# A new head for a fused attention and expert kernel: another order of loads, gates, decays and scores, fillers spread among them, and scores' operands loaded in two parts

## The chip, the core and the metric

The kernel runs on one core of a Trainium2 chip. The core has a matrix engine (TensorE, PE in the profile), three engines for elementwise work (VectorE or DVE, ScalarE or ACT, GpSimd or POOL), a queue that issues transfers (SyncE or SP) and 16 DMA engines. Each engine works through its own list of instructions in order and waits on semaphores for the others. The metric is the time of one execution on the device in microseconds; less is better.

## What is computed

A recurrent attention with gates (2 batches, 8 heads, 768 steps, head size 40) feeds two expert layers in a row, all in float32:

```python
for t in range(S):
    m_new = np.maximum(f_gate[:, :, t] + m, i_gate[:, :, t])
    f_stab = np.exp(f_gate[:, :, t] + m - m_new)
    i_stab = np.exp(i_gate[:, :, t] - m_new)
    m = m_new
    C = f_stab * C + i_stab * einsum('bhd,bhe->bhde', vt, kt)
    n = f_stab * n + i_stab * kt
    y[:, :, t] = sigmoid(o_gate) * (C q_t) / max(|n q_t|, 1)
x = y as 1536 rows of 320
x = ((x @ w_a) * (x @ w_b)) @ w_out      # inner width 1536
out = leaky_relu(x @ w_in) @ w_out2      # inner width 2048
```

The expert weights arrive as float64 and are turned into float32 pieces on the chip.

## The kernel before

The steps of attention are cut into 6 chunks of 128 for each of the 2 batches; a chunk is written `p:b`. Within a chunk the recurrence becomes matrix products: scores (k times q, `score_mm`, step `smm`), a matrix of decays (`decay_scan`, step `dsc`), their product (`score_at`, `sat`), outputs (`out`), and the state carried on (`state_mm`, `stm`). The decays of chunk 0 come from the gates: two scans (`gate_scan`), sums and differences (`gate_fa`, `gate_fb`, `gate_i`), exponentials (`gate_exp`), a split of the result in two parts (`gate_first`), and products that spread a row over all partitions (`decay_mm`, `dmm`). `gate_cums` (`gcum`) makes running products for the later chunks; `store_decays` and `store_cums` write them to memory, from where the later chunks read them.

The outputs are divided by a denominator (`outputs_norm`, three small DVE instructions, step `onm`), multiplied by the output gate (`gate_norm` on POOL, step `og`; `norm` on DVE, step `nrm`), transposed on PE (`x_mm`, step `xmm`) and split into a high part (`x_hi` on ACT, `xh`) and a rest (`x_lo` on DVE, `xl`).

A weight is loaded (`load_raw`, `lw`), decoded from float64 by two ACT instructions (`dh`, `dl`) and a merge on DVE (`dm`), rounded on ACT (`dr`), and its rest taken on POOL (`ds`). The first expert layer then runs in 12 slices: the two up products (`up`, line 559), their product split in two parts (`e1`, `em`, `eh`, `el`), and the down product (`dn`, lines 617 to 619). The second layer does the same with `um`, `v1`, `vh`, `vl` and `dd` (lines 586 and 617 to 619).

Nothing is scheduled by the compiler. The string `ORDER` lists 1116 steps, and each engine's instructions stand in the order in which these steps issue them. `spin` is a step without a result: one product of zeros, 128x512 in bfloat16, which only keeps PE running. Before, 16 of them stand at the start. Each tile pool in the PSUM memory has a few buffers, and a step that needs a buffer waits until its last reader is done: `ps_att` chooses among three pools, `pa` (2 buffers), `mm` (2) and `dn` (4).

Of the kernel before, what the change touches and what calls it, by code (L numbers as in the profile page):

```python
# [7 lines left out]
F32 = mybir.dt.float32  # L8
# [10 lines left out]
B, H, S, D = 2, 8, 768, 40  # L19
# [5 lines left out]
T = 128  # L25
# [12 lines left out]
    dm:2 onm:0:1 dm:4 out:0:0 lc:1 lf:1:0 lw:3 scum dr:4 og:0:1 smm:1:0 dsc:1:0:1 onm:0:0 dh:3 dr:2 dsc:1:0:0
    og:0:0 lw:6 lk:1:0 lq:1:0 ld:1:0 stm:0:0 stm:0:1 ds:4 sat:1:0:0 nrm:0:1 nrm:0:0 lf:1:1 sat:1:0:1 dl:3
    ste:0:1 nd:0:0 ds:2 val:1:0 ste:0:0 nd:0:1 vo:1:0 xmm:0:0 xmm:0:1 xh:0:0 lk:1:1 lw:5 ls:1:1 lw:7 lq:1:1  # L40
    ld:1:1 xh:0:1 xl:0:0 xl:0:1 up:0:1 up:0:0 dm:3 dl:6 dh:6 qry:1:0 dr:3 e1:0:1 e1:0:0 dm:6 em:0:1 em:0:0
    sig:1:0 eh:0:0 eh:0:1 out:1:0 ds:3 el:0:1 onm:1:0 el:0:0 dsc:1:1:1 up:0:3 dr:6 dh:5 sig:1:1 dl:5 val:1:1
    og:1:0 ds:6 vo:1:1 qry:1:1 dm:5 up:0:2 lw:8 e1:0:3 nrm:1:0 em:0:3 dsc:1:1:0 e1:0:2 dn:0:0 smm:1:1 dh:7 dl:7
    dr:5 nd:1:0 sat:1:1:0 sat:1:1:1 em:0:2 dm:7 lk:2:0 lq:2:0 lw:9 eh:0:2 up:0:4 lf:2:0 dl:8 dr:7 eh:0:3 out:1:1
    xmm:1:0 dh:8 key:1:0 ds:5 onm:1:1 dn:0:1 el:0:2 el:0:3 dn:0:2 og:1:1 xh:1:0 e1:0:4 nrm:1:1 xl:1:0 em:0:4
    dm:8 ds:7 dn:0:3 nd:1:1 stm:1:0 xmm:1:1 eh:0:4 dl:9 xh:1:1 up:0:5 dr:8 xl:1:1 ste:1:0 ds:8 e1:0:5 up:1:0
    em:0:5 el:0:4 lw:10 ls:2:0 lk:2:1 vo:2:1 val:2:0 key:1:1 up:1:1 smm:2:0 dh:9 eh:0:5 e1:1:0 dsc:2:0:0 dm:9
# [5 lines left out]
    out:2:0 eh:1:5 dh:13 dr:11 eh:0:6 dr:12 sig:2:0 el:1:5 dsc:3:0:1 e1:0:7 up:1:6 onm:2:0 em:0:7 key:2:1
    ste:2:0 el:0:6 e1:1:6 eh:0:7 dl:13 ds:12 ds:11 val:2:1 og:2:0 up:1:7 dn:0:6 dn:1:5 el:0:7 em:1:6 nrm:2:0
    dm:13 smm:2:1 qry:2:1 stk:1:1 lw:14 lw:16 lf:3:1 up:0:8 dl:15 e1:1:7 eh:1:6 dr:13 sat:2:1:0 dl:14 dh:14
    el:1:6 stk:2:0 ds:13 dl:16 nd:2:0 em:1:7 sat:2:1:1 eh:1:7 dh:15 e1:0:8 dsc:3:1:0 dn:1:6 out:2:1 dn:0:7
    up:0:9 em:0:8 el:1:7 dm:14 dn:1:7 dm:15 stm:2:1 onm:2:1 dsc:3:1:1 dr:14 up:1:8 e1:0:9 eh:0:8 dr:15 og:2:1
# [66 lines left out]
def attention_experts_kernel(ctx: ExitStack, tc: tile.TileContext, gates, consts, stk, kvo, q3, w1, wd1, w2, wd2, out):  # L124
# [35 lines left out]
    idr = c_p.tile([128, 4, 128], F32, name="idr")  # L160
# [173 lines left out]
    def decay_mm(b, hh):  # L334
        p = 0
# [467 lines left out]
```

## Time and profile before

| | |
|---|---|
| median of 3 runs | 456.62 us (456.11 to 456.94) |
| the profiled execution | 455.65 us, of which the span of the engines' work is 453.9 us |
| PE busy, share of the span | 98% |
| DVE, ACT, POOL busy | 46%, 46%, 28% |
| transfers | 47.79 MB, mean 105 GB/s |

A row of the timeline gives the start and the length in microseconds, the engine, the line of the kernel, the operation, the tile written and the tiles read, the shapes and the count; brackets hold the idle time before it and what ended that. A matrix product in float32 may appear as two records (16 of line 372 are 8 products). PE's granted clock is given as a share of its full speed: 1.00 is 2.4 GHz, 0.50 is 1.2 GHz. Before the first change of the clock the table shows 1.00 for want of a record.

### The profile page before, as it was taken

To read this page: it belongs to the slowest core of one execution; us is meant where nothing else is said; L and a number is where in the kernel's file an instruction comes from. 1 tells how busy PE (TensorE), PEld (TensorE's weight loads), DVE (VectorE), ACT (ScalarE), POOL (GpSimd) and SP (SyncE) were. 2 spreads that over 40 slices of the span, in tenths; PEclk is the share of its full clock that TensorE was granted. 3 is DMA by queue.
4 is the path that set the end of the run, shared out by engine and by line. 5 is a ranking of instruction groups with operands and counts; after the bars stand their busy time and mean duration, and the time that the engine had idled before them with its cause. 6 is when DMAs were issued, how large, how long until landed. Compare 5 with 4: busy or idle time off the path is not lost.

```text
span 453.9 us, 7049 instructions
## 1 busy us (share of the span) xinstructions
PE 446.4 (98%) x2774; PEld 404.5 (89%) x2774; DVE 209.3 (46%) x352; ACT 208.2 (46%) x381; POOL 125.5 (28%) x135
## 2 busy tenths in 40 slices
PE   7999999999999999999999999999999999999997
PEld 3989999999988898898888888989899999999896
DVE  5997978677565453343156431342422131131112
ACT  4776756645142223125676655843533343333222
POOL 2678582964412611010314241030300000000000
PEclk9569999999999999999999999999999999999999
DMA  7999997862460410015412534010010000010001
GB/s 245 308 356 289 279 269 219 279 182 57 136 188 27 135 32 2 0 39 241 139 59 63 181 89 155 1 58 1 0 59 0 2 0 1 1 59 0 1 0 59
DMA packets 25998, 47.79 MB, mean 105 GB/s; under 512 B 1801, under 2 KB 18765, under 8 KB 25965
## 3 DMA queue, kind: packets, MB, share of 16 engines
q1 hardware_dynamic: 25965, 47.34, 33.7%
q8 instruction: 22, 0.36, 0.3%
q14 instruction: 11, 0.09, 0.1%
HBM read 45.28 MB, written 2.05 MB: 104 GB/s over the span
## 4 chain that ended last, share of the span: by engine, by line
PE 96%; DMA 1%; DVE 1%; ACT 1%; SPq 0%; issue 0%; POOL 0%; ACTq 0%
PE mm L559 30%; PE mm L586 20%; PE dn L617 11%; PE dn L619 11%; PE dn L618 11%; PE pa L419 4%; PE pa L372 3%; PE pa L414 2%; PE dn L419 2%; PE pa L445 1%; DMA ident_all<-consts 1%; PE pa L490 1%; PE pa L649 1%; PE mm L445 1%; PE dn L372 0%; PE pa L340 0%
## 5 line engine op out<-in xcount | busy, mean ns | idle before, releaser
L559 PE MATMUL mm<-xh,wa 128*128 128x256 f32 (+1 forms) x480 | 114.8, 340 | 0.6 <-ACT xh L504 0.6
L559 PEld LDWEIGHTS mm<-xh,wa 128*128 128x128 f32 x480 | 79.8, 189 | 9.6 <-ACT xh L504 0.8
L602 DVE TENSOR_TENSOR gl<-gg,gh 128x512 fp32r<-128x512 f32 x48 | 34.2, 730 | 99.4 <-ACT gh L597 95.3
L559 PE MATMUL mm<-xl,wa 128*128 128x256 f32 (+1 forms) x288 | 79.3, 337 | 0.0
L592 ACT ACTIVATE gg<-mm 128x512 f32<-128x512 f32 x48 | 28.1, 594 | 72.3 <-PE mm L586 70.9
L617 PE MATMUL dn<-wa,gh 128*128 128x320 f32 x192 | 59.5, 310 | 0.0
L619 PE MATMUL dn<-wa,gl 128*128 128x320 f32 x192 | 59.3, 309 | 0.0
L618 PE MATMUL dn<-wa,gh 128*128 128x320 f32 x192 | 59.2, 309 | 0.0
L559 PEld LDWEIGHTS mm<-xl,wa 128*128 128x128 f32 x288 | 51.1, 189 | 6.0
L564 ACT ACTIVATE gg<-mm 128x256 f32<-128x256 f32 (+1 forms) x48 | 23.4, 487 | 67.0 <-PE mm L559 51.1
L569 DVE TENSOR_TENSOR gg<-gg,mm 128x256 f32<-128x256 f32 (+1 forms) x48 | 26.2, 546 | 59.4 <-PE mm L559 35.3
L617 PE MATMUL dn<-wd,gh 128*128 128x320 f32 x144 | 45.9, 319 | 0.0
L619 PE MATMUL dn<-wd,gl 128*128 128x320 f32 x144 | 44.5, 309 | 0.0
L618 PE MATMUL dn<-wd,gh 128*128 128x320 f32 x144 | 44.4, 309 | 0.0
L578 DVE TENSOR_TENSOR gl<-gg,gh 128x256 fp32r<-128x256 f32 (+1 forms) x48 | 36.0, 753 | 11.7 <-ACT gh L573 11.6
L573 ACT ACTIVATE gh<-gg 128x256 fp32r<-128x256 f32 (+1 forms) x48 | 25.0, 522 | 32.4 <-DVE gg L569 25.4
L597 ACT ACTIVATE gh<-gg 128x512 fp32r<-128x512 f32 x48 | 29.8, 630 | 21.7 <-PE dn L618 21.3
L618 PEld LDWEIGHTS dn<-wa,gh 128*128 128x128 f32 x192 | 36.1, 188 | 1.3
L617 PEld LDWEIGHTS dn<-wa,gh 128*128 128x128 f32 x192 | 36.0, 188 | 1.2
L619 PEld LDWEIGHTS dn<-wa,gl 128*128 128x128 f32 x192 | 36.0, 188 | 0.0
L586 PE MATMUL mm<-yh,wa 128*128 128x512 f32 x120 | 35.8, 395 | 0.0
L586 PE MATMUL mm<-yh,w 128*128 128x512 f32 x120 | 35.6, 394 | 0.0
(110 smaller groups left out, 739.2 us busy)
## 6 DMA issues: line engine op xcount, KB each, us to landing
y<-w SPq DMA_DIRECT2D x12, 768.0 KB
raw<-w SPq DMA_DIRECT2D x8, 768.0 KB
kvo<-kvo SPq DMA_DIRECT2D x12, 484.0 KB
pp<-fdr SPq DMA_DIRECT2D x10, 512.0 KB
raw<-wd SPq DMA_DIRECT2D x8, 640.0 KB
stk<-stk SPq DMA_DIRECT2D x12, 416.0 KB
y<-wd SPq DMA_DIRECT2D x6, 640.0 KB
out<-y SPq DMA_DIRECT2D x12, 160.0 KB
```

The lines of the kernel that those rows point to most:

```text
L419: pe.matmul(ps[:, h * E1:(h + 1) * E1], at_t[p, b, h // 4][:, h % 4, :], v[:, h, :], start=p == 0, stop=p == 0 or h == h0 + nh - 1,)
L559: pe.matmul(halves_[ab], w[:, slot, ab, :], xs[lo][:, kt, cs], start=i == 0, stop=i == 7)
L569: dve.tensor_tensor(out=g, in0=g, in1=up_t.pop((blk, f))[1], op=ALU.mult)
L573: act.activation(out=gh, in_=g_t[blk, f], func=AF.Copy)
L578: dve.tensor_tensor(out=gl, in0=g_t.pop((blk, f)), in1=raw_view(gh_t[1, blk, f]), op=ALU.subtract)
L586: pe.matmul(ps, w[:, slot, f % 2, :], xs[lo][:, kt, :], start=i == 0, stop=i == 7)
L592: act.activation(out=g, in_=ps, func=AF.Prelu, alpha=0.01)
L597: act.activation(out=gh, in_=g_t[2, blk, f], func=AF.Copy)
L602: dve.tensor_tensor(out=gl, in0=g_t.pop((2, blk, f)), in1=raw_view(gh_t[2, blk, f]), op=ALU.subtract)
L617: pe.matmul(ps, gh[:, cs], w[:, 0, :], start=f == 0, stop=False)
L618: pe.matmul(ps, gh[:, cs], w[:, 1, :], start=False, stop=False)
L619: pe.matmul(ps, gl[:, cs], w[:, 0, :], start=False, stop=f == last)
```

## The change

The step table is replaced by one of 1151 steps. The 16 `spin` steps at the start become 51, of which 15 stand before the first transpose and the rest among the products of the head. Gates and decays of chunk 0 now stand ahead of the weights' merges, batch 0 ahead of batch 1; `gcum` stands behind the first two products of scores and decays. The tile of a chunk's scores operands holds two groups of 40 partitions, at 0 and at 64. It was one transfer of 104 partitions, the 24 between them filled with zeros by the host's layout; it becomes two transfers of 40. The steps `gate_ist`, `decay_mm` and `state_mm` take their PSUM buffers from other pools, and so does the fillers' target. The order of all later steps differs too.

```diff
-    lg:0 init spin spin spin spin spin spin spin spin spin spin spin spin spin spin spin spin lg:1 lw:1 lc:0
-    ls:0:1 gs:0 lw:0 lk:0:1 ls:0:0 lw:2 gfa:0 gs:1 gfa:1 sel gfb:0 gfb:1 gi:0 smm:0:1 gi:1 dh:1 idr gef:1 gef:0
+    lg:0 lg:1 lw:0 init gs:0 gfa:0 gfb:0 gi:0 gei:0 gef:0 lc:0 gfr gs:1 gi:1 spin dh:0 gfa:1 dl:0 idr sel spin
+    spin spin spin spin spin spin spin spin spin spin spin spin spin gist:0 ls:0:0 lk:0:1 spin spin dmm:0:0 spin
...
     def load_stk(p, b):
         t = a_p.tile([128, 2, 4, T], F32, tag="stk", name="stk", bufs=3)
-        sp.dma_start(out=t[0:64 + D], in_=stk[b, p])
+        for u in range(2):
+            sp.dma_start(out=t[64 * u:64 * u + D], in_=stk[b, p, u])
         stk_t[p, b] = t
...
     def gate_ist(cc, n):
-        ps = ps_att("mm")
+        ps = ps_att()
...
     def decay_mm(b, hh):
-            src = ps_att("mm" if b and hh else None)
+            src = ps_att()
...
     def state_mm(p, b):
-        ps = ps_att(None if p else "mm")
+        ps = ps_att(None if p else "dn")
...
-    wps = ps_dn.tile([128, 512], F32, tag="dn", name="dn")
+    wps = ps_mm.tile([128, 512], F32, tag="mm", name="mm")
...
-    stk = np.zeros((B, NC, 64 + D, 2, 4, T), np.float32)
-    for u in range(2):
-        stk[:, :, 64 * u:64 * u + D] = qk[:, :, u].transpose(1, 3, 5, 0, 2, 4)
+    stk = qk.transpose(1, 4, 2, 6, 0, 3, 5)
```

Lines of the changed kernel are higher by 1 to 3 (372 becomes 375, 559 becomes 562).

DVE, from the second gate scan on, before: the selector (line 691), the gates' differences (284, 288), the running products (308), the copy of the input gates (323), a weight's merge (231), then scans of the decays (350) and products with the scores (377).

```order
L691 TENSOR_TENSOR sel<-ident_all 64x16
L284 TENSOR_TENSOR wd<-wd 64x128
L284 TENSOR_TENSOR wd<-wd 16x640
L288 TENSOR_TENSOR wd<-wd 16x128
L288 TENSOR_TENSOR wd<-wd 16x640
L308 SCALAR_TENSOR_TENSOR wd<-wd,zero 16x128 x5
L323 COPY istn<-mm 128x16
L231 SCALAR_TENSOR_TENSOR y<-y 128x768
L350 SCALAR_TENSOR_TENSOR pp<-pa,idr 128x512
```

The same place in the changed kernel:

```order
L694 TENSOR_TENSOR sel<-ident_all 64x16
L326 COPY istn<-pa 128x16
L234 SCALAR_TENSOR_TENSOR y<-y 128x768
L287 TENSOR_TENSOR wd<-wd 16x640
L353 SCALAR_TENSOR_TENSOR pp<-pa,idr 128x512 x2
L380 TENSOR_TENSOR at<-dn,pp 128x512 x2
L311 SCALAR_TENSOR_TENSOR wd<-wd,zero 16x128 x5
L353 SCALAR_TENSOR_TENSOR pp<-pa,idr 128x512
```

Of the gates' differences only the long one of the decays is still behind the selector, the merge stands ahead of it, and the five running products stand behind two scans and two products.

PE from the last fillers to the first up product, before: scores (372), input gates (322), decays (340), outputs (419), states (445), transposes (490).

```order
L372 MATMUL dn<-stk 128x128 x8
L322 MATMUL mm<-ident_all,wd 128x16
L340 MATMUL mm<-fr,sel 128x128 x4
L340 MATMUL pa<-fr,sel 128x128 x12
L322 MATMUL mm<-ident_all,wd 128x16 x5
L372 MATMUL dn<-stk 128x128 x8
L419 MATMUL dn<-kvo,at 128x41 x16
L372 MATMUL pa<-stk 128x128 x8
L445 MATMUL mm<-kvo 120x123 x2
...
L490 MATMUL pa<-ident_all,ya 128x128 x6
L559 MATMUL mm<-xh,wa 128x256 x4
```

PE in the changed kernel, from the last transposes of the head on; a pair with `gg` is one filler:

```order
L493 MATMUL pa<-ident_all,ya 128x128 x3
L448 MATMUL dn<-kvo 120x123 x2
L448 MATMUL dn<-kvo 80x82
L331 LDWEIGHTS gg
L331 MATMUL mm<-gg 128x512
L562 MATMUL mm<-xh,wa 128x256 x4
...
L331 LDWEIGHTS gg
L331 MATMUL mm<-gg 128x512
L375 MATMUL pa<-stk 128x128 x8
```

The scores of chunk 1:0 (the third row of 372, now 375) have moved from ahead of the states to behind the first up product, and a filler stands on either side of that product.

DVE at the outputs of chunk 1:1 in the changed kernel, where PE goes from the last output products (422) straight to a down product (620 to 622) that reads this `gl`:

```order
L433 TENSOR_SCALAR den<-pa 128x8
L434 TENSOR_TENSOR den<-den,pa 128x8
L435 RECIPROCAL rec<-den 128x8
L581 TENSOR_TENSOR gl<-gg,gh 128x256
L481 TENSOR_TENSOR ya<-pa,kvo 128x320
```

And PE there, in the changed kernel and then before:

```order
L422 MATMUL pa<-kvo,at 128x41 x2
L620 MATMUL dn<-wd,gh 128x320
L621 MATMUL dn<-wd,gh 128x320
L622 MATMUL dn<-wd,gl 128x320
```

```order
L419 MATMUL pa<-kvo,at 128x41 x2
L490 MATMUL pa<-ident_all,ya 128x128 x3
L617 MATMUL dn<-wd,gh 128x320
L618 MATMUL dn<-wd,gh 128x320
L619 MATMUL dn<-wd,gl 128x320
```

Before, the down products right behind the outputs are those of slice 1 (`dn:0:1`), and those of slice 2 follow; now slice 1 stands earlier, and slice 2 (`dn:0:2`) comes straight behind the outputs.

## Rows read from the trace of the kernel before

**Rows 1.** The page: busy us, share of the span and instructions of each engine.

```profile
PE 446.4 (98%) x2774; PEld 404.5 (89%) x2774; DVE 209.3 (46%) x352; ACT 208.2 (46%) x381; POOL 125.5 (28%) x135
```

**Rows 2.** Windows: length, each engine's busy us, granted clock, DMA share, GB/s.

```profile
9.88:30.36 20.48, 19.83 (x112) 18.57 (x110) 18.81 (x33) 14.49 (x22) 12.99 (x18) 0.50 1.02 331
30.36:100.00 69.64, 69.04 (x580) 67.78 (x580) 54.26 (x97) 44.70 (x85) 49.20 (x48) 1.00 0.87 257
```

**Rows 3.** Windows: the stretch between the fillers and the first scores.

```profile
7.30:9.17 1.87, 0.00 (x0) 0.00 (x1) 1.82 (x5) 1.83 (x4) 0.11 (x1) 1.00 0.98 283
```

**Rows 4.** Timeline of PE, from the first filler to the first up product.

```profile
1.00 6.28 PE L328 MATMUL dn<-gg 128*128 128x512 bf16 x16 [1.00 <-DVE wd L688]
...
9.17 1.53 PE L372 MATMUL dn<-stk 40*128 40x128 f32 x16 [1.90 <-DMA stk<-stk]
...
11.16 1.11 PE L340 MATMUL mm<-fr,sel 64*128 64x128 f32 x4 [0.19 <-POOL fr L296]
...
18.12 7.05 PE L419 MATMUL dn<-kvo,at 128*128 128x41 f32 x32
25.10 2.08 PE L372 MATMUL pa<-stk 40*128 40x128 f32 x16
27.11 2.60 PE L445 MATMUL mm<-kvo 128*120 128x123 f32 x12
...
31.32 0.74 PE L559 MATMUL mm<-xh,wa 128*128 128x256 f32 x4 [0.60 <-ACT xh L504]
```

**Rows 5.** Timeline of DVE in the head.

```profile
7.35 0.17 DVE L691 TENSOR_TENSOR sel<-ident_all 64x16 fp32r<-64x16 f32 x1 [1.55 <-DMA ident_all<-consts]
7.45 1.01 DVE L284 TENSOR_TENSOR wd<-wd 64x128 f32<-64x128 f32 x2
...
9.32 1.91 DVE L308 TENSOR_TENSOR_SCAN wd<-wd,zero 16x128 f32<-16x128 f32 x5
...
11.22 0.94 DVE L231 SCALAR_TENSOR_TENSOR y<-y 128x768 int32<-128x768 int32 x1
13.16 1.22 DVE L350 TENSOR_TENSOR_SCAN pp<-pa,idr 128x512 f32<-128x512 f32 x1 [1.00 <-PE pa L340]
...
20.71 0.69 DVE L377 TENSOR_TENSOR at<-dn,pp 128x512 f32<-128x512 f32 x1
```

**Rows 6.** Timeline of ACT in the head.

```profile
7.03 0.90 ACT L223 ACTIVATE y<-y 128x768 f32<-128x768 f32 x1 [5.00 <-DMA y<-w]
7.83 0.61 ACT L696 ACTIVATE idr<-ident_all 128x512 f32<-128x512 f32 x1
...
12.19 0.89 ACT L240 ACTIVATE wa<-y 128x768 fp32r<-128x768 f32 x1 [0.18 <-DVE y L231]
...
22.65 0.83 ACT L401 ACTIVATE kvo<-kvo 128x320 f32<-128x320 f32 x2
...
30.39 0.87 ACT L504 ACTIVATE xh<-pa 128x384 fp32r<-128x384 f32 x2 [1.16 <-PE pa L490]
```

**Rows 7.** Timeline of POOL: the output gates of chunks 0:1 and 0:0.

```profile
23.27 1.27 POOL L437 TENSOR_TENSOR kvo<-kvo,rec 128x320 f32<-128x320 f32 x1 [1.33 <-DVE rec L432]
26.26 1.46 POOL L437 TENSOR_TENSOR kvo<-kvo,rec 128x320 f32<-128x320 f32 x1 [1.72 <-DMA ddr<-wd]
```

**Rows 8.** Timeline of PE at the full clock: scores of chunk 1:1, last outputs of 1:1.

```profile
42.72 1.16 PE L372 MATMUL pa<-stk 40*128 40x128 f32 x16
...
47.79 0.57 PE L419 MATMUL pa<-kvo,at 128*128 128x41 f32 x4
```

**Rows 9.** Timeline of DVE around those outputs.

```profile
45.72 2.38 DVE L231 SCALAR_TENSOR_TENSOR y<-y 128x768 int32<-128x768 int32 x1
48.40 0.17 DVE L430 TENSOR_SCALAR den<-pa 128x8 f32<-128x8 f32 x1 [0.30 <-PE pa L419]
...
48.92 1.24 DVE L578 TENSOR_TENSOR gl<-gg,gh 128x256 fp32r<-128x256 f32 x2
50.08 0.48 DVE L478 TENSOR_TENSOR ya<-pa,kvo 128x320 f32<-128x320 f32 x1
```

More of the change, by code (lines that the diff above doesn't have):

```diff
@@ L38 @@
[L38 to L47, printed above, removed]
@@ L53 @@
[L53 to L57, printed above, removed]
@@ new lines @@
+    out:0:1 key:0:1 val:1:0 og:0:0 vo:1:0 onm:0:1 dr:1 dh:4 dl:4 dr:2 spin spin spin spin stm:0:1 spin og:0:1
+    spin lw:3 scum spin nrm:0:0 lf:1:0 lq:1:0 lc:1 ld:1:0 ls:1:0 nrm:0:1 dm:4 nd:0:1 dl:3 nd:0:0 ds:1 xmm:0:0
+    spin xmm:0:1 stm:0:0 spin dr:4 dsc:1:0:0 sig:1:0 xh:0:0 xh:0:1 dh:3 xl:0:0 xl:0:1 ste:0:0 dm:3 up:0:0 spin
+    dr:3 e1:0:0 lw:6 ds:2 lf:1:1 smm:1:0 dsc:1:0:1 sat:1:0:0 em:0:0 sat:1:0:1 qry:1:0 ds:4 up:0:1 dh:6 dl:6
+    eh:0:0 e1:0:1 out:1:0 ds:3 dsc:1:1:0 dsc:1:1:1 lk:1:1 lw:5 onm:1:0 em:0:1 dm:6 dl:5 og:1:0 vo:1:1 val:1:1
@@ new lines @@
+    sig:1:1 el:0:0 dr:6 eh:0:1 up:0:3 lq:1:1 ls:1:1 ds:6 nrm:1:0 up:0:2 dn:0:0 smm:1:1 e1:0:3 nd:1:0 el:0:1
+    key:1:0 em:0:3 lw:7 ld:1:1 sat:1:1:0 ste:0:1 e1:0:2 eh:0:3 dl:7 dh:5 dh:7 dn:0:1 xmm:1:0 up:0:4 el:0:3
+    em:0:2 sat:1:1:1 dm:5 dm:7 dr:5 eh:0:2 xh:1:0 dr:7 e1:0:4 qry:1:1 out:1:1 ds:5 xl:1:0 onm:1:1 el:0:2 og:1:1
+    lw:8 nrm:1:1 ds:7 dn:0:2 nd:1:1 dh:8 dl:8 dn:0:3 stm:1:0 xmm:1:1 up:0:5 ste:1:0 em:0:4 dm:8 xh:1:1 eh:0:4
+    dr:8 lw:9 ls:2:0 lf:2:0 lk:2:0 lw:10 xl:1:1 e1:0:5 up:1:0 el:0:4 em:0:5 stk:1:0 ds:8 key:1:1 up:1:1 dl:9
@@ new lines @@
+    nd:2:0 dh:16 e1:0:9 dr:15 stm:2:1 out:2:1 em:0:9 el:0:8 onm:2:1 ste:2:1 eh:0:9 dl:16 ds:14 og:2:1 up:1:8
+    dn:0:8 xmm:2:0 up:1:9 xh:2:0 dsc:3:0:0 nrm:2:1 el:0:9 nd:2:1 e1:1:8 xmm:2:1 dn:1:7 ds:15 em:1:8 xl:2:0
+    up:0:10 lk:3:1 lq:3:0 ld:3:1 qry:3:0 lf:4:0 lq:3:1 dn:0:9 dh:17 eh:1:8 e1:1:9 xh:2:1 el:1:8 em:1:9 ls:3:1
+    lk:4:0 dm:17 xl:2:1 dm:16 eh:1:9 e1:0:10 em:0:10 dr:16 smm:3:0 up:1:10 el:1:9 sat:3:0:1 sat:3:0:0 eh:0:10
+    dr:17 e1:1:10 dn:1:8 stk:2:0 ds:16 key:3:0 vo:4:0 vo:3:1 out:3:0 up:1:11 sig:3:1 em:1:10 ls:4:0 dsc:3:1:0
@@ new lines @@
+    el:0:10 onm:3:0 og:3:0 eh:1:10 e1:1:11 nrm:3:0 smm:3:1 dn:1:9 up:0:11 dsc:3:1:1 em:1:11 sat:3:1:0 el:1:10
+    sat:3:1:1 stm:3:0 stk:2:1 val:3:1 qry:3:1 dsc:4:0:0 ste:3:0 key:3:1 ds:17 e1:0:11 out:3:1 eh:1:11 nd:3:0
+    onm:3:1 og:3:1 nrm:3:1 ls:5:1 lk:4:1 lq:4:0 dn:1:10 ld:4:0 xmm:3:0 dn:0:10 xh:3:0 nd:3:1 el:1:11 em:0:11
+    xl:3:0 xmm:3:1 eh:0:11 xh:3:1 xl:3:1 dn:1:11 stm:3:1 dsc:4:0:1 ste:3:1 up:2:0 lq:4:1 lk:5:0 ls:4:1 lf:4:1
+    e1:2:0 el:0:11 em:2:0 dn:0:11 smm:4:0 stk:3:0 val:4:0 val:5:0 qry:4:0 key:4:0 up:2:1 eh:2:0 ye:0 sig:4:0
@@ new lines @@
+    ye:1 e1:2:1 sat:4:0:0 el:2:0 sat:4:0:1 em:2:1 stm:4:0 out:4:0 up:2:2 dn:2:0 e1:2:2 eh:2:1 el:2:1 dsc:4:1:1
+    ste:4:0 onm:4:0 em:2:2 lq:5:0 lf:5:0 up:2:3 dn:2:1 vo:4:1 og:4:0 stk:3:1 stk:4:0 e1:2:3 eh:2:2 nrm:4:0
+    em:2:3 dsc:4:1:0 el:2:2 up:2:4 dn:2:2 smm:4:1 ls:5:0 ld:4:1 lk:5:1 ld:5:0 lf:5:1 val:4:1 key:4:1 vo:5:1
+    qry:4:1 eh:2:3 sig:4:1 e1:2:4 sat:4:1:1 em:2:4 el:2:3 sat:4:1:0 eh:2:4 nd:4:0 up:2:5 xmm:4:0 xh:4:0 e1:2:5
+    em:2:5 out:4:1 el:2:4 dsc:5:0:0 onm:4:1 up:2:6 dn:2:3 og:4:1 vo:5:0 e1:2:6 eh:2:5 xl:4:0 em:2:6 el:2:5
@@ L108 @@
+    dd:2:14:3 dd:2:15:3
 """
```

107 lines of the change are left out of this document (49 added, 58 removed).

## The prediction, made before the changed kernel had run

> **What bounds the kernel now.** I read the page first: PE is busy 98% of the span and no other engine is above 46% [rows 1]. So the time is PE's list of work, its clock, and the few places where PE waits. The windows come next. From 9.88 to 30.36 us PE is busy 19.83 of 20.48 us, yet at a granted clock of 0.50, the level of 1.2 GHz; from 30.36 to 100 it is busy 69.04 of 69.64 us at 1.00 [rows 2]. Ahead of that PE stood idle from 7.30 to 9.17, for 1.87 us, and the clock fell at 9.88 [rows 3]. The timeline of PE shows what this slow head holds: 16 fillers to 7.28, then a wait of 1.90 us for the first scores' operands, decays, scores, outputs for 7.05 us from 18.12, scores of chunk 1:0 for 2.08, states for 2.60, and the first up product at 31.32, behind a last wait of 0.60 for `xh` [rows 4]. Behind that product PE hardly waits. The kernel is therefore a head of 31.32 us and a body of full PE at the full clock, and whatever moves the first up product moves the end by as much, unless the body gains or loses something of its own.
>
> What holds the head? DVE's timeline: the first scan of decays (line 350) starts at 13.16, after a wait of 1.00 for PE's decay products, and the last product of scores and decays (377) ends at 20.71 + 0.69 = 21.40 [rows 5]. From there to 31.32 PE works off outputs, scores, states and transposes at half clock.
>
> **The change: the chain up to the first scan.** Ahead of everything ACT waits 5.00 us for the first weight, which lands at 7.03 [rows 6]. The change has the gates and one weight of the same size ahead there still, so I leave 7.03 for `lw:0`, the weight whose merge now stands ahead of the first scan on DVE. Two decoding instructions of at most 0.90 each on ACT [rows 6] overlap by some 0.10, so they end near 8.7; the copy `idr`, 0.61, ends at 9.3 and is hidden behind the merge, 0.94 on DVE [rows 5], which ends near 9.6. Then comes the long gate difference: the pair on line 284 takes 1.01 [rows 5], of which I give 0.8 to the one of 640 columns (all 1.01 is the upper bound). First scan: 10.4 in place of 13.16.
>
> **Up to the last product of the head.** From 13.16 to 21.40, 8.24 us, DVE does four scans of 1.22, four products of 0.69, a merge and a small copy, close together [rows 5]. The changed list holds the same between its first scan and its last product, and in addition the five running products, 1.91 us [rows 5], which stood ahead before. 10.4 + 8.24 + 1.91 = 20.5, against 21.40: only 0.9 us of the 2.8 is left at this point. PE must keep up: at the full clock I halve what it does in rows 4 (a filler, 6.28 / 16 = 0.39 at the start, becomes 0.2 as an estimate; the scores at full clock have a row, 1.16 [rows 8], where one chunk took 2.08 [rows 4]). Scores of two chunks, decays, outputs of 3.5 and the fillers between then fit beside DVE's list, and the wait of a decay product for a PSUM buffer still held by a scan is inside DVE's time.
>
> **From there to the first up product.** Now PE's work is behind other engines. A denominator takes 0.52 on DVE, from 48.40 to 48.92 [rows 9]; the list has two of them around a merge of 0.9, to 22.4. The output products in between are four, about 0.8 at most before the second denominator, beside the merge. POOL multiplies the output gates in 1.27 and 1.46 [rows 7]; I take 1.2 behind the second denominator, since nothing but small steps stands ahead of it on POOL: 23.6. The normalizing product on DVE, 0.48 [rows 9]: 24.0. Then ACT's list is what ends last: a merge of 0.94 on DVE must go ahead, 24.9; a rounding of 0.89 on ACT, 25.8; one sigmoid, 0.83 / 2 = 0.42, 26.2; two `xh`, 0.87 together, 27.1 [rows 5, 6, 9]. With a little for semaphores the first up product starts at 27.2, where it was 31.32: **-4.1**. States, transposes and fillers of PE lie beside this chain.
>
> **Given back.** The scores of chunk 1:0 have left the head and stand behind the first up product, at the full clock: 1.16 [rows 8], **+1.1**. The fillers on either side of that product: one on the path, **+0.2**. The first up product's `xl` part waits for `x_lo`, which follows `x_hi`: **+0.2**. Further on, at the outputs of chunk 1:1, PE goes straight from the outputs to a down product that reads a `gl`. On DVE that `gl` stands behind the denominators of the same outputs, so PE must wait for the end of its own outputs, then 0.52 of denominators and one `gl`, 1.24 / 2 = 0.62 [rows 9], and two semaphores; the two products of `gh` ahead of it cover some 0.3. Before, transposes and an earlier slice filled this place. Behind the waiting product stand the rest of slice 2 and the states: **+1.0**. Sum: -4.1 + 1.1 + 0.2 + 0.2 + 1.0 = **-1.6**.
>
> **The load in two parts.** Twelve loads of operands, 4 KB for each partition, carry 320 KB each in place of 416, so DMA moves 12 x 96 KB = 1.15 MB less of 47.79. In the head, where DMA's share is 1.02 at 331 GB/s [rows 2], 96 KB is 0.3 us, some 0.4 with the second load of the head, at most. The other bound is nothing: in the stretch in which such a load was moving, DMA's share was 0.98 but the rate 283 GB/s [rows 3], so such a load doesn't fill the engines it is spread over. I take nothing, since the first scores' place in the new chain is behind `dm:0` and the decays, which don't wait for this load. The Trainium skill, "DMA: Bandwidth & Descriptors", in its section on why a DMA increments its semaphore by 16, says that a transfer is spread over the largest number up to 16 that divides its partitions, on the lowest-numbered engines: 104 partitions would use 13 engines with 8 rows each, 40 use 10, and both parts the same ten, again 8 rows each. By this the two parts land no sooner and the sum stays -1.6; by bytes it is -2.0. The lower rate of that stretch agrees with it as far as it goes.
>
> The order of all later steps differs too. PE's instructions there are the same ones, and 98% busy leaves them little to win; I put nothing, and up to 3 us of loss as a rival.
>
> **The rivals.** (A) The sum: -1.6. On the profiled execution, 455.65, that is 454.05, a span of 452.3; the median shown is 0.97 above the profiled time, so the median is **455.0**. Its own range, with the bounds of loads and differences and the wait at slice 2 between 0 and 2: 454.0 to 455.8.
>
> (B) The clock falls in the thin stretch from the last outputs to the first up product, where PE has fillers, states and transposes in place of solid work. For it: it fell after 1.87 us of idling [rows 3]. Against: the fillers break the idle time up. If it stays at half until about 30.4 as before [rows 2], the up products from 27.2 on run at half for 3.2 us and lose 1.6: 456.6, no change.
>
> (C) The other side. The clock falls before the scores, as it did, and PE's longer list, now with fillers, binds. After 9.88 it holds some 34 fillers at 0.39, 13.3 us, and the products of the old head, 19.83 [rows 2] plus 0.7 of scores ahead of it less 2.08 for chunk 1:0, 18.4: 32 us in all at half. At half to 30.36, 20.5 of these are done; the rest takes 6 at the full clock: first up at 36.4 in place of 31.32, with the 2.5 given back behind it about +7, 463. It decides from about 3 us of half clock on at a place where PE binds. Against it: the first decay products need only the gates, not the scores' operands for which PE waited 1.90 [rows 4], and fillers stand in that gap.
>
> (D) The body loses more. Merges on DVE beside other work take 2.38 [rows 9] where the first took 0.94 [rows 5]; weights loaded later (the second is now issued behind four other loads) come later through decode, merge and rounding, and each up product that waits costs its wait. One to 3 us: 457 to 458.
>
> (E) It goes better: no wait at slice 2, as DVE is far ahead there (-2.6), or POOL's product is off the path as well (-3.4): 453.2 to 454.0.
>
> **How the numbers follow.** A 0.46, B 0.20, C 0.10, D 0.14, E 0.10. What can be told from no change here is about 0.2%, 0.9 us. The range leaves out C and little of D: 453.2 to 458.0. Faster by over 0.2% (below 455.7): nearly all of A and E, 0.52. Within it: B, the lower end of D, a rest of A, 0.28. Slower (above 457.5): C and the upper end of D, 0.20.
>
> **What would show it.** In the changed profile: the first merge ends near 9.6; the first scan starts near 10.4; the last product of scores and decays of the head ends near 20.5; a granted clock of 1.00 from about 6.5 on without a break to the end; the first up product at 27.2, its wait ended by `xh`; an idle time of about 1 us ahead of line 622 behind the outputs of chunk 1:1, ended by `gl`; first scores' operands landing at about 9.1 as before. Wrong it is if the clock row shows 0.50 again after 10, if the first up product is later than 28.5, or if the idle time of PE behind the head adds up to over 2 us more than before.

## The result and the profile after

The changed kernel takes 458.94 us (median of 9 runs, 457.10 to 460.59), the kernel before 456.11 us (9 runs, 455.66 to 456.94). The ratio is 1.0052, 95% interval 1.0034 to 1.0071: slower by half a per cent. The forecast was 455.0 us, faster, in a range of 453.2 to 458.0. The profiled execution of the changed kernel is the fastest of its runs: 457.10 us, span 455.3, against 455.65 and 453.9 before. So there are two things to explain: 1.4 us in the profiled executions, and a median that lies 1.8 us above the changed kernel's own best run, where before it lies 0.5 above.

The windows of [rows 2] in the changed kernel:

```profile
9.88:30.36 20.48, 18.88 (x142) 13.45 (x142) 18.03 (x33) 15.52 (x23) 14.57 (x17) 1.00 0.86 304
30.36:100.00 69.64, 69.15 (x584) 67.49 (x583) 51.83 (x96) 45.13 (x86) 46.01 (x46) 1.00 0.78 244
```

The slow head is gone. The clock is at 1.00 where it was at 0.50, and DMA has a share of 0.86 in place of 1.02. The two bodies, from the first up product to the end, first of the changed kernel, then of the kernel before:

```profile
28.03:455.30 427.27, 421.41 (x2655) 384.39 (x2655) 185.24 (x315) 189.36 (x352) 110.58 (x112) 1.00 0.29 91
```

```profile
31.32:453.90 422.58, 419.19 (x2638) 382.98 (x2638) 184.75 (x307) 188.69 (x352) 109.66 (x112) 1.00 0.30 91
```

The first up product starts 3.29 us sooner (28.03, before 31.32), and the body is 4.69 us longer (427.27, before 422.58): PE is busy for 2.22 us more and idle for 2.47 us more in it. The timeline of PE says where:

```profile
10.30 1.16 PE L375 MATMUL dn<-stk 40*128 40x128 f32 x16
...
19.02 3.77 PE L422 MATMUL dn<-kvo,at 128*128 128x41 f32 x32
...
26.11 0.33 PE L493 MATMUL pa<-ident_all,ya 128*128 128x128 f32 x1 [1.02 <-ACT ya L486]
...
28.03 0.74 PE L562 MATMUL mm<-xh,wa 128*128 128x256 f32 x4 [0.27 <-ACT xh L507]
29.08 0.50 PE L562 MATMUL mm<-xl,wa 128*128 128x256 f32 x2 [0.30 <-DVE xl L513]
...
30.61 0.39 PE L331 MATMUL mm<-gg 128*128 128x512 bf16 x1
30.93 1.16 PE L375 MATMUL pa<-stk 40*128 40x128 f32 x16
...
49.15 0.41 PE L622 MATMUL dn<-wd,gl 128*128 128x320 f32 x1 [0.49 <-DVE gl L581]
...
119.65 0.46 PE L417 MATMUL pa<-ct,q 120*128 120x123 f32 x2 [1.52 <-DVE at L380]
```

Read against [rows 4]: the transposes wait 1.02 for a copy on ACT. Behind the first up product PE waits 0.30 for `xl`, then come a filler (30.61 to 30.93, 0.32) and the scores of chunk 1:0 (30.93 to 32.02, 1.09), which had left the head. At 49.15 stands the wait for `gl` that the prediction had named, with 0.49. At 119.65 stands one that it had not: the outputs of chunk 3:1 wait 1.52 for a product of scores and decays. The waits of 0.30, 0.49 and 1.52 make 2.31 of the 2.47 us of idle time; the filler and the scores make 1.41 of the 2.22 us of work. The other 0.8 us of PE's busy time is spread over the body in small pieces, and no run here takes it apart.

DVE in the head of the changed kernel, and at the late wait:

```profile
8.25 0.96 DVE L234 SCALAR_TENSOR_TENSOR y<-y 128x768 int32<-128x768 int32 x1
...
9.86 2.32 DVE L353 TENSOR_TENSOR_SCAN pp<-pa,idr 128x512 f32<-128x512 f32 x2
...
19.68 0.68 DVE L380 TENSOR_TENSOR at<-dn,pp 128x512 f32<-128x512 f32 x1
21.04 0.17 DVE L433 TENSOR_SCALAR den<-dn 128x8 f32<-128x8 f32 x1 [0.68 <-PE dn L422]
...
22.83 0.17 DVE L433 TENSOR_SCALAR den<-dn 128x8 f32<-128x8 f32 x1 [0.48 <-PE dn L422]
...
110.08 0.40 DVE L581 TENSOR_TENSOR gl<-gg,gh 128x256 fp32r<-128x256 f32 x1
...
114.81 0.68 DVE L380 TENSOR_TENSOR at<-pa,pp 128x512 f32<-128x512 f32 x1
115.41 3.49 DVE L581 TENSOR_TENSOR gl<-gg,gh 128x256 fp32r<-128x256 f32 x1
118.82 0.68 DVE L380 TENSOR_TENSOR at<-pa,pp 128x512 f32<-128x512 f32 x1
```

The first merge, the first scan and the last product of the head (at 8.25, 9.86 and 19.68) are within 0.6 us of where the prediction put them. Then DVE waits 0.68 and 0.48 for PE's outputs. At 115.41 a `gl` of 128x256, which takes 0.40 at 110.08, takes 3.49, between the two products (line 380) on which the outputs hang.

### The profile page after: what moved, and what is told of

It reads as the page before. It is cut to its first block, busy times and chain, and to the rows that moved or that the text cites. A ratio compares the mean times of both kernels' runs of the same rounds, so it can differ in the third digit from the quotient of the medians.

```text
span 455.3 us, 7141 instructions
## 1 busy us (share of the span) xinstructions
PE 446.7 (98%) x2809; PEld 399.5 (88%) x2809; DVE 207.7 (46%) x352; ACT 208.4 (46%) x381; POOL 125.9 (28%) x135
## 4 chain that ended last, share of the span: by engine, by line
PE 89%; DMA 4%; DVE 3%; issue 1%; POOL 1%; ACT 1%; SPq 0%; DVEq 0%; POOLq 0%
PE mm L562 28%; PE mm L589 19%; PE dn L620 11%; PE dn L622 11%; PE dn L621 11%; PE pa L422 3%; PE pa L375 2%; DMA fdr<-wd 2%; PE pa L417 2%; DMA y<-w 1%; DMA q<-q 1%; PE pa L448 1%; PE pa L652 1%; DVE gl L581 1%; PE pa L493 1%
## 5 line engine op out<-in xcount | busy, mean ns | idle before, releaser
L605 DVE TENSOR_TENSOR gl<-gg,gh 128x512 fp32r<-128x512 f32 x48 | 32.0, 689 | 101.0 <-ACT gh L600 101.0
L595 ACT ACTIVATE gg<-mm 128x512 f32<-128x512 f32 x48 | 28.2, 595 | 64.6 <-PE mm L589 61.7
L589 PE MATMUL mm<-yh,w 128*128 128x512 f32 x120 | 35.5, 393 | 0.0
```

What stands on the lines that cost most here:

```text
L589: pe.matmul(ps, w[:, slot, f % 2, :], xs[lo][:, kt, :], start=i == 0, stop=i == 7)
L595: act.activation(out=g, in_=ps, func=AF.Prelu, alpha=0.01)
L605: dve.tensor_tensor(out=gl, in0=g_t.pop((2, blk, f)), in1=raw_view(gh_t[2, blk, f]), op=ALU.subtract)
```

## The experiments

Each version ran beside the kernel before on the same chip; a ratio is to that, with its 95% interval. Versions that ran on different chips are compared by their ratios, and the medians are given beside them. "Mean clock" is the granted clock of one run, averaged over its span: it is 0.977 for the kernel before, whose head of 20.5 us at 0.50 gives just that, and 1.000 for a run that never falls after the start. The theories that the expectations name: **Theory 1**, PE's waits in the reordered body cost their own length and no more; **Theory 2**, the clock falls in most executions, in the head or behind a wait, and the products that follow run at half.

**The load in two parts, each way alone.** `one_load` undoes it in the changed kernel, `two_loads` puts it into the kernel before.

```diff
-        for u in range(2):
-            sp.dma_start(out=t[64 * u:64 * u + D], in_=stk[b, p, u])
+        sp.dma_start(out=t[0:64 + D], in_=stk[b, p])
...
```

> The changed kernel with the scores' operands loaded in one transfer of 104 partitions again. If the load in two parts does nothing, the median stays at 458.9 within 0.9 and the first scores start when they did (10.30 us), since DVE's chain and not this load sets their place. If the 96 KB saved per load count, it is 0.4 to 1 us slower.

> The kernel before with the load in two parts and nothing else changed. PE waits 1.90 us for this load there, so a sooner landing shows at once: by bytes (320 of 416 KB) the wait shrinks by some 0.3 to 0.5 us and the median goes from 456.1 to 455.7; if both parts go over the same few DMA engines it stays at 456.1, wait 1.90.

`one_load`: 458.92 us (7 runs), ratio 1.0050 [1.0028, 1.0072], where the changed kernel has 1.0052; its first scores start at 10.76, not at 10.30 as expected. `two_loads`: 455.91 (12 runs), ratio 0.9984 [0.9970, 0.9997]. The first scores of `two_loads`:

```profile
8.02 0.48 PE L373 MATMUL dn<-stk 40*128 40x128 f32 x2 [1.11 <-DMA stk<-stk]
9.00 2.03 PE L373 MATMUL dn<-stk 40*128 40x128 f32 x14 [0.49 <-DMA stk<-stk]
```

The first part is there for the products at 8.02, the second for those at 9.00, where the whole load let PE start at 9.17 [rows 4]. By bytes all would have been there 0.3 to 0.5 sooner. The Trainium skill's rule ("DMA: Bandwidth & Descriptors", the section on why a DMA increments its semaphore by 16), by which both parts lie on the same ten engines with as many rows on each as before, says no sooner. The 0.17 does not decide between them: `body_only` below, with the whole load and the same head, starts these scores at 9.80, so one execution differs from another by more. In `two_loads` the first up product starts 0.32 sooner (31.00), and the span is no shorter (454.0, before 453.9); the ratio puts the gain at 0.0 to 0.3%.

In the changed kernel the medians show nothing. The profiled execution of `one_load` has its first up product 0.43 later (28.46): its first product on the identity tile waits 1.97 for another transfer, `ident_all`, which DVE has at 7.95. With the load in two parts DVE has it between 6.71 and 7.60, so that up to 0.4 us for the load's form is neither shown nor excluded.

**Head and body apart.** `head_only` has the changed order up to the first up product and a filler, and from there on what is left in the order before; `body_only` the reverse.

```diff
 head_only: ... xl:0:0 xl:0:1 ste:0:0 dm:3 up:0:0 spin
-    dr:3 e1:0:0 lw:6 ds:2 lf:1:1 smm:1:0 dsc:1:0:1 sat:1:0:0 em:0:0 sat:1:0:1 qry:1:0 ds:4 up:0:1 ...
+    smm:1:0 dsc:1:0:1 lw:6 ds:4 sat:1:0:0 lf:1:1 sat:1:0:1 ste:0:1 ds:2 lk:1:1 lw:5 ls:1:1 lw:7 ...
```

> The changed kernel's steps up to and including its first up product and one filler, then the remaining steps in the order of the kernel before. Theory 1 (the new order of the later steps costs what the head wins: waits of PE at 48 and 119 us, and late scores): profiled first up near 28, profiled span 2 to 3 us below the changed kernel's 455.3, about 452.5 to 453.5. Theory 2 (the clock falls in the head's thin stretch in most executions): the median stays 1 to 3 us above the best of its runs, the mean granted clock near 0.991, and the median is 456 to 457.5.

> The kernel before up to its second up product, then the remaining steps in the changed order. Theory 1: slower than before by 1.5 to 3 us, 457.6 to 459, with PE waiting at the outputs of chunk 1:1 and near 120 us as in the changed kernel. Theory 2 (only the head and its clock cost): 456.1 within 0.9, and all runs at a mean clock of 0.977 and close together.

`head_only`: 455.63 us (12 runs, 455.36 to 456.74), ratio 0.9976 [0.9962, 0.9990]: the new head, with the changed loads and buffers, makes the median less. The profiled span does not show it: 454.0, where the kernel before has 453.9 and Theory 1 had 452.5 to 453.5. The difference of the medians lies in the clock, since the kernel before has executions that fall further: of the 24 beside `head_only` nine have a mean clock of 0.970 to 0.974, and they take 456.84 to 458.45 us. Nor is Theory 2's mean clock of 0.991 there: it is 0.992 to 1.000. `body_only`: 462.38 us (6 runs), ratio 1.0114 [1.0090, 1.0138], slower than either theory had it. Its profile shows a part of the reason; first PE, then windows around it:

```profile
52.72 0.45 PE L615 MATMUL dn<-wd,gl 128*128 128x320 f32 x1 [0.62 <-DVE gl L574]
52.97 0.46 PE L613 MATMUL dn<-wd,gh 128*128 128x320 f32 x1
```

```profile
53.00:54.00 1.00, 1.00 (x5) 1.00 (x5) 0.49 (x1) 0.19 (x2) 0.92 (x2) 0.50 1.16 376
...
56.00:57.00 1.00, 1.00 (x10) 1.00 (x10) 0.37 (x2) 0.05 (x1) 0.00 (x0) 0.81 1.06 326
```

PE waits 0.62 for the same `gl`, and from 53 to some 56.4 us the clock stands at 0.50: down products follow each other at 0.27 us in place of 0.15. A wait of 0.62 us has cost some 1.5 us behind itself, an estimate from these distances. The wait near 120 us is there too (1.47 at 124.76), and the clock did not fall behind it. Most of the rest is in the head, whose steps are those of the kernel before: the first scores started at 9.80, the first up product at 31.95, and the half clock lasted to 35.5 us, past the first up products, in place of 30.4.

`head_only` keeps nothing in its span of its first up product, which starts at 28.13, 3.19 sooner than before. 1.7 of that go to the scores, the filler and the wait for `xl`; a further 0.7 or so goes here, PE and then DVE (the rest in small pieces that no run takes apart):

```profile
41.69 0.48 PE L371 MATMUL pa<-stk 40*128 40x128 f32 x2
42.51 1.13 PE L371 MATMUL pa<-stk 40*128 40x128 f32 x14 [0.33 <-issue]
```

```profile
40.70 1.31 DVE L230 SCALAR_TENSOR_TENSOR y<-y 128x640 int32<-128x640 int32 x1
41.93 0.48 DVE L477 TENSOR_TENSOR ya<-pa,kvo 128x320 f32<-128x320 f32 x1
```

The scores of chunk 1:1 stop after two products (41.69) until 42.51. Their second PSUM buffer is read by the normalizing product (line 477), which stands behind a merge of 1.31 on DVE and ends at 42.41.

> head_only with two edits: the product that normalizes chunk 1:0 (nrm:1:0) stands ahead of a weight's merge (dm:5) on DVE, since it frees the PSUM buffer for which PE waited 0.9 us in the scores of chunk 1:1 near 41.6, and the filler behind the first up product is left out. Theory 1 (each costs its own time on PE): 0.7 + 0.3 less, median 454.6 against head_only's 455.6. If something that comes later by the merge's move makes PE wait again, 455.6 within 0.5.

```diff
-    ... up:0:0 spin smm:1:0 ... vo:1:1 qry:1:1 dm:5 up:0:2 lw:8 e1:0:3 nrm:1:0 em:0:3 ...
+    ... up:0:0 smm:1:0 ... vo:1:1 qry:1:1 up:0:2 lw:8 e1:0:3 nrm:1:0 dm:5 em:0:3 ...
```

`head_nrm2`: 455.33 us (12 runs, 455.24 to 456.54), ratio 0.9960 [0.9945, 0.9975], the lowest median of the study; the scores run through from 41.60. The edit also leaves out the filler behind the first up product, so the two are not told apart. In the profiled spans it is 0.5 less than `head_only` (453.5, 454.0), in the medians 0.3, where 1.0 was expected.

**The two waits of the body.** `fix_119` moves one step on DVE, `fix_48` another.

```diff
 fix_119
-    ... sat:3:1:0 el:1:10 sat:3:1:1 ...
+    ... sat:3:1:0 sat:3:1:1 el:1:10 ...
 fix_48
-    ... eh:0:2 xh:1:0 dr:7 ... out:1:1 ds:5 xl:1:0 onm:1:1 el:0:2 og:1:1 ...
+    ... eh:0:2 el:0:2 xh:1:0 dr:7 ... out:1:1 ds:5 xl:1:0 onm:1:1 og:1:1 ...
```

> The changed kernel with one step moved: the rest gl that stands between the two products of scores and decays of chunk 3:1 (el:1:10) goes behind them, so the 3.49 us that it takes there beside POOL's work no longer hold up PE's outputs. Theory 1: the 1.52 us of waiting near 119.6 go and the median falls by 1.5, to 457.4 within 0.9. Theory 2 (the clock falls behind that wait too): it falls by 2.5 to 3, to 456 to 456.5, with a higher mean clock. If gl's length moves on to another step that PE waits for, nothing is gained: 458.9.

> The changed kernel with one step moved: the rest gl of slice 2 (el:0:2) stands on DVE ahead of the denominators of chunk 1:1's outputs, so PE doesn't wait there. Theory 1 (a wait on PE costs its own length): the 0.49 us of waiting near 48.6 go, the median falls by 0.5, to 458.4 within 0.9. Theory 2 (the clock falls behind that wait in most executions, as in body_only, where it stood at 0.50 from 53 to 56.4 us): the median falls by 1.5 to 2, to about 457.2, the runs come closer together, and most runs have a mean granted clock of 0.995 or more in place of 0.991.

`fix_119`: 455.80 us (12 runs, 455.43 to 457.43), ratio 0.9978 [0.9962, 0.9994]. One step moved turns the changed kernel from slower into faster than before: 0.74% between the two ratios, 3.4 us (3.1 between the medians), for a wait of 1.52 us. The profiled span falls by 1.6 (453.7), the wait itself; the rest is in the clock. Of the changed kernel's nine runs one has a mean clock of 0.998 and the others 0.989 to 0.993; of `fix_119`'s twelve six have 1.000.

That the clock falls because of this wait is borne out by counts, not by a trace of each run. The step that moved stands at 119 us and cannot change what the clock did in the head. With this head and the wait, in the changed kernel, `one_load`, `fix_48` and `after_look`, 3 of 23 runs have a mean clock of 0.998 or more; with this head and without the wait, in `fix_119`, `fix_both` and `pool_early`, 21 of 36. Against it stands `no_fill`: it has the wait (1.5), and its six runs at 0.972 to 0.974 have about the mean clock that its slow head alone gives (24 us at 0.50 make 0.974).

`fix_48`: 460.47 us (6 runs), ratio 1.0072 [1.0047, 1.0098]: a miss. The wait went elsewhere. DVE and then PE:

```profile
48.11 1.59 DVE L577 TENSOR_TENSOR gl<-gg,gh 128x256 fp32r<-128x256 f32 x1 [0.33 <-ACT gh L572]
```

```profile
53.73 0.50 PE L558 MATMUL mm<-xh,wa 128*128 128x256 f32 x2 [0.81 <-POOL wa L245]
```

At its new place `gl` takes 1.59 in place of the 0.37 that it took behind the denominators, beside work on POOL, and the denominators and the POOL work that waits for them come 1.9 us later than in the changed kernel (part of it since PE itself stands later there); PE then waits 0.81 at an up product for a weight's rest from POOL. (It also waits 0.88 at 39.57, ahead of the moved step. In this execution the clock had also fallen in the head, from 22.9 to 26.3, so the two traces do not stand in step.) The wait of 1.52 stayed, as did the clock's falls: one of its six runs has 0.996, one 0.995, four 0.989.

> fix_119, and the states of chunk 1:0 (stm:1:0, some 1.0 us on PE) ahead of the down product that waits for gl behind the outputs of chunk 1:1, so that they fill that wait. Theory 1: 0.5 less than fix_119's 455.8, 455.3. If the clock in the slower ones of fix_119's runs (0.992) fell behind this wait, those runs go as well and the runs lie within 0.8 of each other. If the states wait there for something of their own, 455.8 or more.

```diff
-    ... nrm:1:1 ds:7 dn:0:2 nd:1:1 dh:8 dl:8 dn:0:3 stm:1:0 xmm:1:1 ...
+    ... nrm:1:1 ds:7 stm:1:0 dn:0:2 nd:1:1 dh:8 dl:8 dn:0:3 xmm:1:1 ...
```

`fix_both` fills the wait of 0.49 at 49.15 from PE's side, on top of `fix_119`: 455.45 us (12 runs, 455.32 to 455.96), ratio 0.9968 [0.9953, 0.9984]. The `gl` product no longer waits; a wait of 0.49 for a weight's rest from POOL has come at 52.07. Nine of twelve runs have a mean clock of 1.000, the other three 0.996, and they lie within 0.64 us.

**What made `gl` long.** `pool_early` leaves DVE's order alone and moves a step of POOL.

```diff
-    ... stk:2:0 ds:16 key:3:0 vo:4:0 vo:3:1 out:3:0 ...   key:3:1 ds:17 e1:0:11 out:3:1 ...
+    ... stk:2:0 ds:16 key:3:0 vo:4:0 vo:3:1 ds:17 out:3:0 ...   key:3:1 e1:0:11 out:3:1 ...
```

> The changed kernel with one step of POOL moved and nothing on DVE: the rest of the last down weight (ds:17, 1.57 us) goes from the row of POOL work beside the long gl of slice 10 into POOL's idle time of 3.5 us ahead of 112 us. If that gl (3.49 us) is long because it stands still until POOL's row of work is through, POOL is done 1.57 us sooner, gl takes about 1.9, the second product of scores and decays follows by 118.0, PE's wait of 1.52 is gone and the median falls as with fix_119, to 455.8 within 0.7. If gl is long for another reason, it stays at 3.49, the wait at 1.5, and the median at 458.9.

POOL in the changed kernel, then POOL and DVE in `pool_early`:

```profile
114.69 0.72 POOL L395 TENSOR_TENSOR kvo<-kvo,istn 128x320 f32<-128x320 f32 x1
115.37 1.01 POOL L362 TENSOR_TENSOR q<-q,db 120x384 f32<-120x384 f32 x1
116.34 0.74 POOL L410 TENSOR_TENSOR kvo<-kvo,pp 128x320 f32<-128x320 f32 x1
117.04 1.57 POOL L258 TENSOR_TENSOR wd<-y,wd 128x640 fp32r<-128x640 f32 x1
```

```profile
117.27 1.01 POOL L358 TENSOR_TENSOR q<-q,db 120x384 f32<-120x384 f32 x1
118.24 0.73 POOL L406 TENSOR_TENSOR kvo<-kvo,pp 128x320 f32<-128x320 f32 x1
```

```profile
117.31 1.95 DVE L577 TENSOR_TENSOR gl<-gg,gh 128x256 fp32r<-128x256 f32 x1
119.18 0.68 DVE L376 TENSOR_TENSOR at<-pa,pp 128x512 f32<-128x512 f32 x1
```

In the changed kernel POOL works without a break from 114.69 to 118.61, and `gl` ends at 118.90, 0.29 behind it. In `pool_early` POOL's row ends at 118.24 + 0.73 = 118.97, and `gl`, started at 117.31, ends at 119.26, again 0.29 behind. It takes 1.95, PE's wait is gone, and the median is 455.90 (12 runs, ratio 0.9995 [0.9981, 1.0009]): as fast as the kernel before, and 0.57% below the changed kernel. (In this profiled execution the clock had fallen in the head, from 21.8 to 28.6, so its times stand some 1.9 us later.) In `fix_119` the same `gl`, behind both products, takes 2.90 and ends at 118.98, 0.30 behind POOL's row. So POOL's work sets when `gl` ends.

It is not always the whole row. DVE and POOL of the changed kernel, earlier:

```profile
39.07 0.94 DVE L581 TENSOR_TENSOR gl<-gg,gh 128x256 fp32r<-128x256 f32 x1
```

```profile
38.28 1.45 POOL L440 TENSOR_TENSOR kvo<-kvo,rec 128x320 f32<-128x320 f32 x1
39.68 0.39 POOL L400 COPY kvo<-istn 128x8 f32<-128x8 f32 x1
40.03 0.72 POOL L395 TENSOR_TENSOR kvo<-kvo,istn 128x320 f32<-128x320 f32 x1
```

This `gl` ends at 40.01, 0.28 behind the first multiplication (39.73), though POOL goes on. The Trainium skill, "SBUF — State Buffer", section "Who interferes with whom", says that DVE with two inputs from SBUF contends with a GpSimd instruction that reads SBUF, that the ports they share are an exclusive lock, and that the order of issue decides who blocks. This agrees with the rows at 39.07, where `gl` outlasted one instruction; in the late place it outlasted three POOL instructions in a row in the changed kernel, and two in `pool_early`. What decides between one and a row is not shown.

**The fillers.** `no_fill` is the changed kernel without the 36 behind the first transpose.

> The changed kernel without the 36 fillers that stand behind the first transpose; the 15 at the start stay. If the fillers hold the clock: it falls to 0.50 in the head as before, PE's list takes up to twice as long, first up product at 29 to 31, median 460 to 462. If the head hangs on DVE and ACT alone: first up at 27.5 to 28, clock or not, median within 1 of 458.9.

Its windows:

```profile
9.88:30.36 20.48, 18.00 (x96) 16.60 (x94) 16.64 (x30) 15.37 (x23) 13.19 (x16) 0.50 0.80 275
30.36:33.00 2.64, 2.64 (x14) 2.54 (x12) 2.52 (x5) 0.93 (x1) 2.64 (x2) 0.52 0.97 330
```

459.81 us (6 runs, 459.39 to 460.27), ratio 1.0062 [1.0040, 1.0083]. The clock stands at 0.50 to nearly 33 us and the first up product starts at 29.41, 1.4 later than with fillers; its profiled run is 2.3 us above that of the changed kernel. But the ratios differ by 0.1% only, less than their intervals: the changed kernel's clock falls in most executions as well, there or behind the late wait:

> The changed kernel once more, unchanged, for a second trace. Theory 2 (the clock falls behind a wait of PE in most executions): if its mean clock is near 0.991, the windows show 0.50 for some 3.4 us right behind 120 us or 48.6 us, and the products there at nearly double their distance, 1.7 us lost for each such stretch. If it falls ahead of 28 us, it costs nothing, since PE waits there anyway.

`after_look`, the same kernel again, took 460.02 us, mean clock 0.989. Windows, then PE:

```profile
21.80:28.20 6.40, 6.40 (x25) 4.64 (x26) 4.43 (x8) 3.48 (x7) 4.84 (x6) 0.50 0.69 213
...
123.90:127.40 3.50, 3.50 (x16) 3.42 (x16) 2.25 (x7) 1.03 (x3) 2.57 (x4) 0.51 0.36 104
```

```profile
29.59 0.74 PE L562 MATMUL mm<-xh,wa 128*128 128x256 f32 x4
...
121.22 0.46 PE L417 MATMUL pa<-ct,q 120*128 120x123 f32 x2 [1.50 <-DVE at L380]
...
124.36 0.47 PE L620 MATMUL dn<-wd,gh 128*128 128x320 f32 x1
124.63 0.47 PE L621 MATMUL dn<-wd,gh 128*128 128x320 f32 x1
```

The clock stands at 0.50 from 21.8 to 28.2, in which PE is busy all the time, with output products, fillers, states and transposes. The first up product starts at 29.59, 1.56 later than in the profiled execution. It falls again at 123.9, 2.7 us behind the wait of 1.50, to 127.4, and down products follow each other at 0.27. The two together are the 2.9 us by which this span (458.2) is longer than the other.

**A still sooner first up product.** `head_xh` is `head_nrm2` with `x_hi` ahead of other work on ACT.

```diff
-    ... nd:0:1 dl:3 nd:0:0 ds:1 xmm:0:0 spin xmm:0:1 stm:0:0 spin dr:4 dsc:1:0:0 sig:1:0 xh:0:0 xh:0:1 dh:3 xl:0:0 ...
+    ... nd:0:0 nd:0:1 ds:1 xmm:0:0 spin xmm:0:1 stm:0:0 spin dsc:1:0:0 xh:0:0 xh:0:1 dh:3 dl:3 dr:4 sig:1:0 xl:0:0 ...
```

> head_nrm2 with three steps of ACT (a decoding, a rounding and a sigmoid) moved from ahead of the x_hi of chunk 0 to behind it, and the copy for chunk 0:0 ahead of that for 0:1. The first up product starts 1.2 to 1.6 us sooner, near 26.7. If the end hangs on the start of the up products, the median falls by as much, to 454. If what comes next isn't there yet (the rest xl on DVE, the operands of chunk 1:0's scores, which DMA brings), PE waits there instead and the median stays at 455.3 within 0.4.

458.99 us (12 runs, 457.13 to 462.42), ratio 1.0065 [1.0035, 1.0096]. PE in it:

```profile
26.43 0.74 PE L558 MATMUL mm<-xh,wa 128*128 128x256 f32 x4
29.20 0.50 PE L558 MATMUL mm<-xl,wa 128*128 128x256 f32 x2 [2.02 <-DVE xl L509]
...
31.10 2.08 PE L371 MATMUL pa<-stk 40*128 40x128 f32 x16
```

The first up product starts 1.55 us sooner than in `head_nrm2` (27.98) and PE then waits 2.02 for `xl`, which stands behind a merge and a scan of 2.32 on DVE. The clock falls to 0.50 from 30.6 to 37.4, over the scores (2.08 in place of 1.16) and the up products. The wait has only changed its place, as was expected; that it would cost 1.05% between the two ratios, 4.8 us (3.7 between the medians), was not.

## Why the prediction was wrong, point by point

- **The chain up to the last product was right, within 0.6 us.** Weight at 6.54 (predicted 7.03), first merge to 9.21 (9.6), first scan at 9.86 (10.4), last product to 20.36 (20.5).
- **From there to the first up product, 27.2, it was 0.8 short** (28.03). The sum had no term for DVE's waits of 0.68 and 0.48 for outputs that PE starts only at 19.02, behind five fillers and the transposes of the input gates: the second denominator ends at 23.43 in place of 22.4, and the later steps keep that lag (the merge ends at 25.86 in place of 24.9, `xh` at 27.98 in place of 27.1). Beside this chain a copy for the transposes (line 486) comes behind a decoding of 0.96 on ACT, so that PE waits 1.02. `head_xh` took that copy and `x_hi` forward together, and the first up product came at 26.43; what the copy alone is worth is not shown.
- **Given back: right terms.** Scores 1.09 (1.1), filler 0.32 (0.2), `xl` 0.30 (0.2), wait at slice 2 0.49 (1.0).
- **The load in two parts: not contradicted.** It was put at nothing, and the median of `one_load` (458.92) agrees. Its profiled execution leaves up to 0.4 us open.
- **The step that failed: "PE's instructions there are the same ones, and 98% busy leaves them little to win; I put nothing".** The same instructions in another order on DVE and POOL put a `gl` between two products on which outputs hang, beside a row of POOL work. This is worth 1.5 us in the profiled execution and, between the ratios of the changed kernel and `fix_119`, 3.4 us in all. The 1 to 3 us of rival D had the size, but not this mechanism: neither late weights nor long merges did it. `fix_119` on DVE and `pool_early` on POOL each take it away with one step. Of the signs of being wrong, the one of over 2 us more idle time of PE behind the head came true (2.47).
- **Rival B had the clock fall in the head alone.** In the profiled execution it holds from 6.5 us on, as forecast; of the nine runs eight have a lower mean clock. The one further execution that was traced, `after_look`, fell in the head at 21.8 and behind the late wait as well: 1.6 us for the head, 1.3 behind the wait. By the counts above, most executions with this head and without the late wait show no fall (21 of 36), and few with it (3 of 23). So what the sum of most executions lacked is chiefly a fall behind a wait in the body, which no rival had.
- **The sign.** With head -3.3, given back 1.7, wait at slice 2 0.5, the late wait 1.5 and 0.8 of small pieces of PE work the profiled sum is about +1.2, measured +1.4; the falls of the clock, less the smaller ones that the kernel before has too, give the rest of the 2.8 us between the medians. Without the late wait the medians are below those of the kernel before by 0.2 to 0.4% in `fix_119`, `fix_both`, `head_only` and `head_nrm2`, and not clear of it in `pool_early` (0.05%). Their best executions gain less: the profiled spans of these four are 453.5 to 454.0, against 453.9. The rest of the gain goes with the clock, which in the kernel before falls further in some executions. So the forecast gain of 1.6 us in the span is not there even without the late wait.

What stays open: the 0.8 us of PE work spread over the body; which share of the clock's falls in the nine runs lay in the head and which behind the wait, since only one of these executions was traced; and why `gl` was held by a whole row of POOL work in one place and by one instruction in another.

## What to carry to other kernels

A new order is priced place by place: look at each engine that feeds the one that binds, and for each wait that the new order can make ask what stands between its producer and the producer's last input. A wait of the matrix engine can cost about twice its length, because the clock may fall behind it (1.50 us of waiting and 1.3 behind it in `after_look`); moving one instruction was worth more here (0.74%) than the whole new head (0.24%). And a gain at the head is kept only if each thing that the next stage needs (operands, buffers, the second half of a split) comes forward as well: `head_xh` brought one of them 1.55 us forward and lost 3.7 in the median.

## What the hardware showed

- The granted clock fell to 0.50 behind waits of PE of 0.62 (`body_only`, 53 to 56.4 us) and 1.50 us (`after_look`, 123.9 to 127.4), with PE busy before and after. Waits of 0.49 and 1.52 passed without a fall in the changed kernel's profiled execution. The runs of that one kernel differ by up to 3.5 us, at mean clocks of 0.989 to 0.998.
- It also fell in a stretch in which PE was busy 6.40 of 6.40 us, with fillers and small products (`after_look`, 21.8 to 28.2). Fillers made a fall rarer, they did not exclude it: without them the mean clock was 0.972 to 0.974 in six of six runs, with them it was 0.998 or more in 24 of the 59 runs counted above.
- An elementwise instruction of DVE with both inputs in SBUF took 3.49 us in place of 0.40 beside an unbroken row of POOL instructions, and ended 0.29 us behind the last of them; in `pool_early` (1.95) and `fix_119` (2.90) it was 0.29 and 0.30. In another place (39.07) it took 0.94 and ended 0.28 behind one POOL instruction, with POOL going on.
